# A convolution and soft-MoE kernel on one core: the last two output stores are issued as seven stores of fewer partitions

## The chip, the cores and the metric

The kernel runs on one NeuronCore of a Trainium2 chip. The metric is the device time of one execution in microseconds. The output goes from SBUF to HBM by DMAs that the SyncE engine (SP) issues on one queue; 16 DMA engines of the core carry them out.

## What is computed

An input `x` of 8 sequences of 3584 tokens with 192 channels goes through a dynamic convolution of 7 taps, whose weights are a softmax of `weight_gen` per token and head, and then through a soft mixture of experts with 32 slots. The lines that matter are these:

```python
w = softmax(weight_gen)                          # over the 7 taps
out = np.einsum('bshk,bskhg->bshg', w, x_unf)    # the convolution
...
logits = x @ phi
slot_input = softmax(logits, axis=0).T @ x       # dispatch: over all 28672 tokens
slot_out[e] = relu(slot_input[e] @ w1[e]) @ w2[e]
c = softmax(logits, axis=1)
return c @ slot_out                              # combine: 28672 x 192 floats
```

All of it is float32. The result is about 22 MB.

## The kernel before

The kernel has two long phases. In the first, up to about 229 us, the input is loaded, convolved on TensorE, transposed, multiplied with `phi`, and reduced into the slots. The loads of `x` go into 32 partitions each, those of the tap weights and of the expert weights into 128. Then a short middle part computes the experts.

The second phase writes the output. It is cut into 25 parts, listed by `out_order()`; the list is `parts`. A part is a piece of one batch (the first 128 channels, `kind` 0) or of two batches (their last 64 channels, `kind` 1) over 18 or 17 groups of 104 tokens. For each part `rows` makes the matmuls of TensorE (line 990), `evict` copies the four PSUM quarters into one region of SBUF (a `spot`) with ScalarE and VectorE (line 996), and `store` issues the DMA on SP (line 1001). A part after the first three is one store of 128 partitions, each partition one contiguous run of `4 * n * 26` floats: 7488 bytes for 18 groups, 7072 bytes for 17. The partition's runs lie behind one another in the output buffer, and the host puts them in order. The first three parts are two smaller stores each, so there are 28 stores.

A planner (`op`, `times`) sets the order of the instructions on the engines; on SP the stores go out in the order of `parts`. A store waits for the copies that fill its spot. Completion of a DMA is counted on one of eight semaphores in turn (called DMAHW0 to DMAHW7 below), and a DMA waits for the one that used its semaphore before, eight DMAs earlier. Behind the last store SP waits for all DMAs that are still out (line 1143), and then the program ends.

The function in question is `store`, with `j` the part's number, `n` its groups, and `lo`, `hi` its quarters; `left[0]` is the place in the output.

Of the kernel before, what the change touches and what calls it, by code (L numbers as in the profile page):

```python
# [17 lines left out]
T = 26  # L18
# [38 lines left out]
def conv_soft_moe(ctx, tc, xh, wh, phi, w1a, w1b, w2, out):  # L57
    nc = tc.nc
    V, A, G, P, SY = nc.vector, nc.scalar, nc.gpsimd, nc.tensor, nc.sync
# [639 lines left out]
    k = SLOTS - 2  # L699
# [125 lines left out]
    for i in sorted(range(len(ops)), key=lambda i: (at[i], i)):  # L825
        if ops[i][5] is loadw2 and ops[i][6] in later:
            continue
        n = len(block.instructions)
# [5 lines left out]
        elif ops[i][0] == SP and at[i] > PACED:  # L834
            to = max((t, k) for k, (t, _) in enumerate(steps) if t <= at[i])[1]
# [138 lines left out]
    spots = [w1flat[:, i * OW : (i + 1) * OW] for i in range(E * F // OW)]  # L974
# [5 lines left out]
    parts = list(out_order())  # L980
    pos, left = {}, [0]
# [12 lines left out]
    def evict(j, n, lo, hi, copy):  # L994
        to = spots[j % len(spots)][:, lo * n * T : hi * n * T]
        copy(to.rearrange("p (q c) -> p q c", c=n * T),  # L996
             pos[j][lo // 2][:, lo % 2 : lo % 2 + hi - lo, 0 : n * T])

    def store(j, n, lo, hi):
        w = (hi - lo) * n * T  # L1000
        SY.dma_start(out[128 * left[0] : 128 * (left[0] + w)].rearrange("(p c) -> p c", p=128),
                     spots[j % len(spots)][:, lo * n * T : hi * n * T])
        left[0] += w

    extra = []
# [20 lines left out]
    def turn_two():  # L1026
        twos[0] += 1
        return ("two", twos[0] % 4)

    for j, (kind, b, g, n) in enumerate(parts):  # L1030
        two, to = [turn_two(), turn_two()], ("spot", j % len(spots))
        op(TE, (1.1 + 0.8 * kind) * (n + 6) / 24, [("cT", 2 * (b + half) + (g >= STEPS[1][0])) for half in range(1 + kind)]
           + ["sob"] * kind, two, rows, kind, b, g, n, j)
        cuts = ((0, 2, AC), (2, 4, VE)) if j < 3 else ((0, 2, AC), (3, 4, VE), (2, 3, AC))
        free = ["w2"] * (j >= RESTAT + 2)
        for lo, hi, e in cuts:
            if e == AC:
                op(AC, 0.14 + 0.4 * (hi - lo) * n / 18, [two[lo // 2], *free], [(to, lo)], evict, j, n, lo, hi, A.copy)
            else:
                op(VE, 0.12 + 0.52 * (hi - lo) * n / 18, [two[1], *free], [(to, lo), ("ev", j)], evict, j, n, lo, hi, V.tensor_copy)  # L1040
        if 4 <= j + 2 < EARLY + 3:
            op(VE, 0.74, [("ev", j)], [("cT", j + 2)], turn, (j + 2) // 2, j % 2)
        for lo, hi in ((0, 2), (2, 4)) if j < 3 else ((0, 4),):
            op(SP, 0.576 * (hi - lo) * n / 18, [], [(to, c[0]) for c in cuts if lo <= c[0] < hi],
               store, j, n, lo, hi, late=2.0)
        if j == RESTAT:
            rest = turn_two()
            op(TE, 1.05, [], [rest], others, 0)
        elif j == RESTAT + 1:
            op(TE, 1.05, [], [rest, "w2"], others, 1)  # L1050
            op(AC, 0.22, [rest], ["sos"], lambda: A.copy(sos[:, DA:D], extra[0][:, 0]))
            op(TE, 0.4, ["sos"], [rest], other_sums)
            op(VE, 0.22, [rest], ["sob"], lambda: V.tensor_copy(sob, extra[0][:, 1]))
# [5 lines left out]
def out_order():  # L1059

    cut = ((0, 18), (18, 17))
    for kind, e in ((0, 0), (0, 1), (0, 2), (0, 3), (1, 0), (0, 4), (1, 2), (0, 5), (0, 6),
                    (1, 4), (0, 7), (1, 6)):
        for g, n in cut:
            if (kind, e, g) == (0, 0, 0):
                yield from ((0, 0, 0, 9), (0, 0, 9, 9))
            else:
                yield kind, e, g, n
# [79 lines left out]
```

## Time and profile before

| what | value |
|---|---|
| three runs | 296.55, 294.46, 296.4 us; median 296.4 us |
| span of the profiled execution | 295.2 us, from the first to the last instruction |
| the output phase | first store issued at 235.6 us, last one at 283.3 us |
| last copy into SBUF | ends at about 283.3 us |
| last bytes of the output leave | about 293.9 us |
| busy shares over the span | PE 88%, DVE 72%, ACT 61%, POOL 54% |

The profile's page gives the busy share of each engine over the whole span and, in 40 equal slices of 7.4 us, the busy share of the engines and of the 16 DMA engines in tenths. A packet in the DMA views is one contiguous run of a transfer, here one partition's row; packets of four bytes are the marks that a DMA engine writes when it has finished its share of a DMA.

### The profile page before, as it was taken

What the parts mean: (1) busy time and instruction counts of PE and PEld (TensorE: products, weight loads), DVE (VectorE), ACT (ScalarE), POOL (GpSimd) and SP (SyncE); (2) the same over time, 40 slices, a digit from 0 to 9 for tenths busy, and PEclk for the clock granted to TensorE, in tenths of its full rate; (3) what the DMA queues carried; (4) which work ended last, traced back from release to release, by engine and by line L of the source; (5) the groups of instructions that cost most, each with busy time, mean ns of one, the idle gap of its engine ahead of it and who ended that gap; (6) DMA issues with size and microseconds to landing.
All of it is one profiled execution on the core that took longest, in us unless ns stands there. A gap on an engine that the chain in (4) does not pass through costs nothing.

```text
span 295.2 us, 16119 instructions
## 1 busy us (share of the span) xinstructions
PE 259.5 (88%) x6996; PEld 210.5 (71%) x6996; DVE 213.2 (72%) x385; ACT 180.4 (61%) x307; POOL 160.1 (54%) x253
## 2 busy tenths in 40 slices
PE   8799999999999999989999999999999797956510
PEld 4578988998997898879899988888869552312100
DVE  8776988887997878676859787773278498977310
ACT  8866657665766666655575666665222378967430
POOL 9975858578686684656465736720036316454100
PEclk9999999999999999999999999999999999967775
DMA  6885776677767766775777758675889099999994
GB/s 188 231 221 154 222 213 188 174 229 199 217 171 228 198 196 178 228 201 161 197 219 220 207 162 232 196 205 168 277 267 297 15 370 414 418 415 414 415 420 174
DMA packets 31558, 70.11 MB, mean 237 GB/s; under 512 B 5888, under 2 KB 21248, under 8 KB 31488
## 3 DMA queue, kind: packets, MB, share of 16 engines
q1 hardware_dynamic: 31488, 69.08, 73.9%
q8 instruction: 55, 0.90, 1.3%
q14 instruction: 15, 0.12, 0.1%
HBM read 46.70 MB, written 22.36 MB: 234 GB/s over the span
## 4 chain that ended last, share of the span: by engine, by line
PE 77%; DMA 6%; issue 4%; DVE 4%; POOL 2%; ACT 2%; ACTq 0%; POOLq 0%; DVEq 0%
PE ring L263 34%; PE ring L283 17%; PE ls L339 8%; PE acb L417 8%; PE two L990 5%; DMA out<-big 4%; PE ring L900 2%; ACT big L996 1%; DMA big<-w 1%; DVE cT L475 1%; POOL LT L106 1%; PE ring L922 1%; POOL big L433 1%; DVE big L433 1%; PE acb L365 1%
## 5 line engine op out<-in xcount | busy, mean ns | idle before, releaser
L263 PE MATMUL ring<-big,band 128*26 128x96 f32 x4480 | 113.1, 248 | 4.8 <-issue 2.9
L263 PEld LDWEIGHTS ring<-big,band 128*26 128x26 f32 x4480 | 101.4, 130 | 15.4 <-issue 8.6
L271 ACT COPY tm<-ring 128x768 f32<-128x768 f32 x68 | 54.4, 800 | 63.2 <-PE ring L263 42.3
L236 DVE STREAM_TRANSPOSE band<-wide 128x832 f32<-128x832 f32 x70 | 70.5, 1025 | 3.8 <-POOL wide L227 2.5
L283 PE MATMUL ring<-ident,tm 122*128 122x122 f32 x408 | 50.5, 273 | 0.5 <-issue 0.5
L227 POOL TENSOR_TENSOR wide<-taps,sum 128x364 f32<-128x364 f32 x32 | 31.4, 982 | 26.6 <-DVE sum L218 13.5
L289 ACT COPY cm<-ring 128x624 f32<-128x624 f32 x68 | 44.1, 690 | 1.6 <-PE ring L283 1.4
L283 PEld LDWEIGHTS ring<-ident,tm 122*128 122x128 f32 x408 | 42.2, 141 | 3.5 <-issue 0.6
L196 POOL TENSOR_TENSOR taps<-taps,top 128x364 f32<-128x364 f32 x34 | 32.9, 974 | 4.3 <-DVE top L188 4.3
L212 POOL TENSOR_TENSOR si<-taps 128x208 f32<-128x208 f32 x34 | 21.7, 637 | 21.5 <-ACT taps L204 20.8
L990 PE MATMUL two<-cT,so 32*128 32x442 f32 (+2 forms) x136 | 22.3, 665 | 12.4 <-DVE cT L475 7.0
L188 DVE TENSOR_REDUCE top<-taps 128x52 f32<-128x364 f32 x34 | 27.8, 821 | 1.3 <-DMA taps<-wh 1.3
L417 PE MATMUL acb<-tm,dt 128*32 128x193 f32 x544 | 26.9, 328 | 0.7 <-issue 0.4
L339 PE MATMUL ls<-cm,phi_sb 128*32 128x208 f32 x544 | 27.4, 338 | 0.0
L94 POOL TENSOR_TENSOR LT<-LT,rm 128x576 f32<-128x576 f32 (+1 forms) x16 | 18.1, 1131 | 16.9 <-DVE rm L92 16.8
L106 POOL TENSOR_TENSOR LT<-LT,sm 128x576 f32<-128x576 f32 (+1 forms) x16 | 18.1, 1133 | 16.7 <-DVE sm L104 16.7
L990 PEld LDWEIGHTS two<-cT,so 32*128 32x128 f32 x136 | 8.6, 212 | 23.1 <-ACT big L996 6.5
L218 DVE RECIPROCAL sum<-sum 128x52 f32<-128x52 f32 (+1 forms) x36 | 16.4, 455 | 10.7 <-POOL sum L214 10.5
L204 ACT ACTIVATE taps<-taps 128x364 f32<-128x364 f32 (+1 forms) x36 | 17.8, 502 | 6.6 <-POOL taps L196 6.5
L339 PEld LDWEIGHTS ls<-cm,phi_sb 128*32 128x32 f32 x544 | 18.2, 109 | 3.7
L417 PEld LDWEIGHTS acb<-tm,dt 128*32 128x32 f32 x544 | 17.2, 110 | 4.9 <-issue 1.3
L346 DVE TENSOR_REDUCE mx<-ls 128x1 f32<-128x416 f32 x17 | 9.9, 585 | 14.6 <-PE ls L339 12.6
(135 smaller groups left out, 297.5 us busy)
## 6 DMA issues: line engine op xcount, KB each, us to landing
big<-xh SPq DMA_DIRECT2D x224, 120.0 KB, 3.5
taps<-wh SPq DMA_DIRECT2D x35, 182.0 KB, 3.6
out<-big SPq DMA_DIRECT2D x7, 884.0 KB, 9.8
big<-w SPq DMA_DIRECT2D x32, 192.0 KB, 3.9
out<-big SPq DMA_DIRECT2D x6, 936.0 KB, 10.4
w1a_sb<-w1a SPq DMA_DIRECT2D x32, 128.0 KB, 3.4
out<-w1a_sb SPq DMA_DIRECT2D x3, 936.0 KB, 12.1
w1b_sb<-w1b SPq DMA_DIRECT2D x16, 128.0 KB, 3.5
```

What stands on the lines that cost most here:

```text
L188: V.tensor_reduce(out=row(m), in_=run(c, 0, KT).rearrange("p k s -> p s k"), axis=AX.X, op=ALU.max)
L196: eng.tensor_tensor(out=t, in0=t, in1=rows7(tops.pop((c, 0))), op=ALU.subtract)
L212: eng.tensor_tensor(out=fold, in0=run(c, 0, 4), in1=run(c, 4, 8), op=ALU.add)
L227: eng.tensor_tensor(out=dst, in0=raw[c % NTAP][:, 0:KT], in1=m.unsqueeze(1).to_broadcast([128, KT, n, T]), op=ALU.mult)
L236: V.transpose(bands[c % NBAND][:, b].rearrange("p b j l -> p (b j l)"), wide[:, b].rearrange("p b j -> p (b j)"))
L263: P.matmul(cv[32 * blk : 32 * blk + T, p % 2, o : o + 4 * GW], bands[g // 8 % NBAND][:, g // 4 % CH, :, i], xbd[:, place(t), :, b * GW : ( ...
L271: copy(tms[tm_at(u)][:, pr + of.start : pr + of.stop, 1 : 2 * D + 1], cv[:, of, 0 : 2 * D])
L283: P.transpose(pt[:, j // 3, o : o + TR], tm[0:TR, pr + j // 3, 1 + o : 129 + o], ident[0:TR, 0:TR])
L289: copy(cm.rearrange("p (a i) (b j) -> p a (i b) j", i=3, j=T), pts["t", k][:, of, 0 : 3 * 128].rearrange("p a (i j) -> p a i j", j=32)[... ...
L339: P.matmul(lp[32 * blk : 32 * blk + 32, lo:hi, par, 0:T], phi_sb[:, 2 * par + i, :], cm[:, lo:hi, 1 if i else 2 * par, blk, :], start=(i = ...
L417: P.matmul(ac[32 * q : 32 * q + 32], dt[:, g, :], tm[:, g // 2, o : o + D + 1], start=(g < 4), stop=(g + 4 >= 2 * n))
L990: P.matmul(pos[j][q // 2][m * half : m * half + m, q % 2, 0 : n * T], of[32 * q : 32 * q + 32], cT[32 * q : 32 * q + 32, g0 : g0 + n, 0:T] ...
```

## The change

The last two parts are stored in pieces. The last but one (part 23, rows of 7488 bytes) goes out as 120 partitions and then the remaining 8; the last one (part 24, rows of 7072 bytes) as 64, 30, 14, 12 and 8. The bytes, their places and the order of partitions are the same; every other store stays one DMA of 128 partitions.

```diff
+    SHARES = {len(parts) - 2: (120, 8), len(parts) - 1: (64, 30, 14, 12, 8)}
+
     def store(j, n, lo, hi):
         w = (hi - lo) * n * T
-        SY.dma_start(out[128 * left[0] : 128 * (left[0] + w)].rearrange("(p c) -> p c", p=128),
-                     spots[j % len(spots)][:, lo * n * T : hi * n * T])
+        to = out[128 * left[0] : 128 * (left[0] + w)].rearrange("(p c) -> p c", p=128)
+        p = 0
+        for k in SHARES.get(j, (128,)):
+            SY.dma_start(to[p : p + k], spots[j % len(spots)][p : p + k, lo * n * T : hi * n * T])
+            p += k
         left[0] += w
```

The order of instructions differs on SP alone, at the end of the program. Before, the last stores on SP stand so (partitions x floats, and the semaphores that each waits for, without their values):

```order
363 L1001 DMA out<-big 128x1872 [waits DMAHW2_49,Activation_49]
364 L1001 DMA out<-big 128x1768 [waits DMAHW3_49,Activation_49]
365 L1001 DMA out<-big 128x1872 [waits DMAHW4_49,Activation_49]
366 L1001 DMA out<-big 128x1768 [waits DMAHW5_49,Activation_49]
367 L1001 DMA out<-big 128x1872 [waits DMAHW6_49,Activation_49]
368 L1001 DMA out<-big 128x1768 [waits DMAHW7_49,Activation_49]
369 L1143 UNCONDITIONAL_BRANCH
```

Now the same place in the program reads:

```order
363 L1006 DMA out<-big 128x1872 [waits DMAHW2_49,Activation_49]
364 L1006 DMA out<-big 128x1768 [waits DMAHW3_49,Activation_49]
365 L1006 DMA out<-big 128x1872 [waits DMAHW4_49,Activation_49]
366 L1006 DMA out<-big 128x1768 [waits DMAHW5_49,Activation_49]
367 L1006 DMA out<-big 120x1872 [waits DMAHW6_49,Activation_49]
368 L1006 DMA out<-big 8x1872 [waits DMAHW7_49]
369 L1006 DMA out<-big 64x1768 [waits DMAHW0_49,Activation_49]
370 L1006 DMA out<-big 30x1768 [waits DMAHW1_49]
371 L1006 DMA out<-big 14x1768 [waits DMAHW2_49]
372 L1006 DMA out<-big 12x1768 [waits DMAHW3_49]
373 L1006 DMA out<-big 8x1768 [waits DMAHW4_49]
374 L1148 UNCONDITIONAL_BRANCH
```

Two stores became seven. The last three pieces wait for the semaphores DMAHW2 to DMAHW4, that is for the completion of the stores in rows 363 to 365 of the same list; nothing else moved on any engine.

## Rows read from the trace of the kernel before

**Rows 1.** The page: span; the 40 slices of DMA share and rate

```profile
span 295.2 us, 16119 instructions
...
DMA  6885776677767766775777758675889099999994
GB/s 188 231 221 154 222 213 188 174 229 199 217 171 228 198 196 178 228 201 161 197 219 220 207 162 232 196 205 168 277 267 297 15 370 414 418 415 414 415 420 174
```

**Rows 2.** Stretches: start:end, length, engines' busy us, PEclk, DMA share, GB/s

```profile
250.00:281.00 31.00, 20.34 (x166) 6.70 (x160) 21.36 (x39) 22.69 (x40) 13.08 (x12) 0.78 1.01 416
281.00:288.00 7.00, 0.23 (x8) 0.00 (x0) 0.91 (x2) 2.25 (x4) 0.00 (x0) 0.70 1.01 416
288.00:290.30 2.30, 0.00 (x0) 0.00 (x0) 0.00 (x0) 0.00 (x0) 0.00 (x0) 0.50 1.04 428
290.60:291.30 0.70, 0.00 (x0) 0.00 (x0) 0.00 (x0) 0.00 (x0) 0.00 (x0) 0.50 0.27 112
292.50:293.80 1.30, 0.00 (x0) 0.00 (x0) 0.00 (x0) 0.00 (x0) 0.00 (x0) 0.50 0.07 27
293.90:295.20 1.30, 0.00 (x0) 0.00 (x0) 0.00 (x0) 0.00 (x0) 0.00 (x0) 0.50 0.00 0
```

**Rows 3.** Waits on SP from 283 us: in total, times, longest

```profile
SPq L1143 <- DMA out<-big: 10.5, 5, 2.3
```

**Rows 4.** DMA packets in 290.3:290.6, 291.3:291.45, 292.1:292.45, 293.8:294.5 us; marks: under 512 B

```profile
DMA packets 17, 0.04 MB, mean 143 GB/s; under 512 B 11, under 2 KB 11, under 8 KB 17
DMA packets 4, 0.02 MB, mean 144 GB/s; under 512 B 1, under 2 KB 1, under 8 KB 4
DMA packets 5, 0.01 MB, mean 40 GB/s; under 512 B 3, under 2 KB 3, under 8 KB 5
DMA packets 1, 0.00 MB, mean 0 GB/s; under 512 B 1, under 2 KB 1, under 8 KB 1
```

**Rows 5.** DMA in 292.45:294.5 us: packets, MB; share of 16 engines

```profile
DMA packets 6, 0.04 MB, mean 17 GB/s; under 512 B 1, under 2 KB 1, under 8 KB 6
...
q1 hardware_dynamic: 6, 0.04, 4.2%
```

**Rows 6.** The same four counts one store earlier: 288.2:288.42, 289.1:289.25, 290.0:290.28, 291.6:291.8 us

```profile
DMA packets 26, 0.11 MB, mean 488 GB/s; under 512 B 11, under 2 KB 11, under 8 KB 26
DMA packets 12, 0.08 MB, mean 524 GB/s; under 512 B 1, under 2 KB 1, under 8 KB 12
DMA packets 20, 0.12 MB, mean 431 GB/s; under 512 B 3, under 2 KB 3, under 8 KB 20
DMA packets 4, 0.02 MB, mean 106 GB/s; under 512 B 1, under 2 KB 1, under 8 KB 4
```

**Rows 7.** DMA in 271.5:273 and in 280.2:281.2 us: the queues of instruction fetches

```profile
q8 instruction: 1, 0.02, 3.7%
...
q14 instruction: 1, 0.01, 1.9%
```

**Rows 8.** The stores from `big` on SP: count, issue in ns (min/median/max), first and last start

```profile
L1001 SPq DMA_DIRECT2D out<-big x13: 332/332/421, 246.6 to 283.3; - x13
```

**Rows 9.** DMA issues at 275.3, at 283.3, and in 235:236.5 us: KB, us to landing

```profile
out<-big SPq DMA_DIRECT2D x1, 936.0 KB, 12.4
out<-big SPq DMA_DIRECT2D x1, 884.0 KB, 11.1
...
out<-w1a_sb SPq DMA_DIRECT2D x2, 234.0 KB, 2.4
```

**Rows 10.** DMA in 5:11 us: packets; share of 16 engines; what was issued

```profile
DMA packets 679, 1.41 MB, mean 236 GB/s; under 512 B 167, under 2 KB 399, under 8 KB 679
...
q1 hardware_dynamic: 679, 1.41, 86.6%
...
big<-xh SPq DMA_DIRECT2D x10, 120.0 KB, 3.3
```

**Rows 11.** DMA in 222:229 us: share of 16 engines; what was issued

```profile
q1 hardware_dynamic: 1500, 2.05, 89.4%
...
big<-w SPq DMA_DIRECT2D x7, 192.0 KB, 4.2
```

## Prediction

> **What bounds the kernel now.** I read the page's slices first: from the 33rd slice on, the 16 DMA engines are 90% busy or more and move 414 to 420 GB/s, until the last slice, where share and rate fall to 4 tenths and 174 GB/s [rows 1]. So the end belongs to the stores. The view by stretches says the same more closely: from 250 to 290.3 us the DMA share is 1.01 to 1.04 (a full queue on every engine), and from 288 us no compute engine does anything [rows 2]. Then the tail is not full: 0.27 of 16 engines, about four, are at work from 290.6 to 291.3 us, 0.07 (one engine) from 292.5 to 293.8 us, none after 293.9 us. SP meanwhile only waits for DMAs, 10.5 us in five waits, at the line behind the program [rows 3]. What sets the end is thus not the amount of output but the slowest of the 16 engines.
>
> How uneven they are can be counted from the marks, packets of four bytes that an engine writes when its share of a store is done. Of the last store's 16 marks, 11 come by 290.6 us, one by 291.45, three by 292.45, and one after 293.8 [rows 4]. One store earlier the same count is 11, 1, 3 and 1, with the last 3.3 to 3.5 us behind the first [rows 6], so these lags are there before the last two stores and no longer grow. Some lag comes from instruction fetches on the same engines: a 16 KB one at about 272 us took 3.7% of 16 engines over 1.5 us, or 0.89 us of one engine, and one more falls between 280.2 and 281.2 us [rows 7]. No row gives an engine a name.
>
> **The price of a row.** After the three late marks one engine moves five rows of 7072 bytes and its mark: 4.2% of 16 engines over 2.05 us [rows 5] is 1.38 us, so 0.275 us a row; in proportion 0.291 us for 7488 bytes. Alone it is no faster than the average engine was under full load: 416 GB/s over 1.01 times 16 engines is 25.7 GB/s, or 0.275 us for 7072 bytes [rows 2]. So a row taken off the last engine shortens the end by that much, and one put on an engine that is in time costs nothing while it stays ahead of the last.
>
> **What the pieces do.** A store of 128 rows gives each of 16 engines 8 rows: its 16 marks are counted above. No transfer in this trace has a number of rows that 16 doesn't divide, so how 120, 30, 14, 12 and 8 rows are dealt is not shown. Two ends bound it: equal shares on the largest number of engines, up to 16, that divides the rows, always beginning at the same first engine; or a spread over all 16 as even as it can be. The second moves at most a row from one engine to another, 0.3 us either way. I take the first, because every transfer that the trace has gives equal shares. Then the 120 rows leave out engine 16, the 8 go one each to engines 1 to 8, the 64 go four to each, the 30 two each to 1 to 15, and the 14, 12 and 8 one each to the first 14, 12 and 8. Over both stores engines 1 to 8 get 18 rows in place of 16, engines 9 to 12 still 16, engines 13 and 14 15, engine 15 14, and engine 16 four. [...]
>
> In time: engine 16 loses 8 rows of 0.291 and 4 of 0.275, 3.43 us. Engines 1 to 8 gain one row of each, 0.57 us. Engines 13 and 14 lose 0.28 us and engine 15 loses 0.55 us.
>
> **The sum.** I take the one that ends at 293.9 us to be engine 16. That is a choice: one engine stands clearly apart, by the same distance two stores running [rows 4, 6], and a lasting handicap fits a fixed place at an end of the deal better than one in its middle. It then ends at 293.9 - 3.4 = 290.5 us. The three that end by 292.4 us are next. If places are evenly likely among the fifteen left, at least one of the three lies among the first eight with 1 - (7 x 6 x 5)/(15 x 14 x 13) = 0.92, so the end is 292.4 + 0.57 = 293.0 us. From the last mark to the end of the span take the same 295.2 - 293.9 = 1.3 us [rows 1, 2] (the landing of the last mark, SP's last wait, the closing barrier). The span becomes 294.3 us, 0.9 us less. Were all three outside the first eight it would be 293.7 us, and with perfectly even ends (0.9 + 3 x 1.8 + 3.4 = 9.7 us of lag, 0.6 us on each of 16) 292.4 us: that is the most there is to win.
>
> **What the extra DMAs cost.** SP issues five more. An issue takes 332 to 421 ns [rows 8], so 1.7 to 2.1 us in all; work in the queue hides them, since the last store is issued at 283.3 us and lands 11.1 us later [rows 9]. The last piece also waits for the semaphore of the store issued at 275.3 us, which lands 12.4 us later [rows 9], at 287.7 us. A store onto idle queues lands 2.4 us after its issue, its data's time included [rows 9], so this piece could be done by 287.7 + 0.4 + 2.4 = 290.5 us; engines 1 to 8 reach its row no sooner than 290.6 + 0.57 - 0.28 = 290.9 us. The margin of 0.4 us is a lower bound. If the cover were gone each us of lateness would show on engines 1 to 8 alone, which are ahead of the 293.0 us end by 1.8 us, except a late one. Five more sets of marks take about 0.01 us each; behind the pieces on SP stands only the closing wait.
>
> **Rival A, the last engine is not the one relieved.** Then the end moves with its place: 293.9 + 0.57, a span of 295.8 us, if it is one of the first eight; 295.2 us on 9 to 12; 294.7 to 294.9 us on 13 to 15. An even spread of the pieces belongs here, 294.9 to 295.5 us. For it: no row names the engine. Against it: the lasting lag. [...]
>
> **Rival B, rows of few partitions go slower.** This is the one that ends slower than before. The trace's transfers into 32 partitions, with few others between, carry 1.41 MB in 6 us at 86.6% of 16 engines, 17.0 GB/s an engine [rows 10]; loads into 128 partitions 2.05 MB in 7 us at 89.4%, 20.5 GB/s [rows 11]; stores from 128 25.7 GB/s [rows 2]. So few partitions may cost a factor of 1.20 (against other loads) up to 1.51 (against stores). Engines 1 to 8 move one row of 0.291 and nine of 0.275 us in such pieces, 2.77 us; the factor adds 0.55 to 1.4 us. The end becomes 293.6 to 294.4 us and the span 294.9 to 295.7 us. It decides from a factor of 1 + 0.9/2.77 = 1.33. If 120 partitions are slowed as well, 8 x 0.291 us adds another 0.5 to 1.2 us, up to 296.9 us. Against it: the 32-partition rows are loads with their own latency, and the late engines move their last rows when others have finished. [...]
>
> **How the numbers follow.** The forecast has 0.5, rival A 0.27, rival B 0.23. The profiled span of 295.2 us is 1.2 us below the median of the runs, 296.4 us; I carry the difference over, so 294.3 becomes 295.5 us. The low end is that of even ends, 2.8 us less than before: 296.4 - 2.8 = 293.6 us, which also covers the lowest run of before less the 0.9 us. The high end is rival A's or B's 0.5 to 0.6 us above before: 297.0 us. Left out are the slowed 120 partitions. A measurement of this kernel can tell about 1%, 3 us, from no change; the largest possible gain is 2.8 us, so faster by over 1% gets 0.06, slower by over 1% (B with more than its rows show) 0.04, and within 1% 0.90.
>
> **What would show it.** In the profile after: marks of the last pieces within about 2.5 us rather than 3.5; one engine alone at the end for less than 0.7 us; SP's closing waits shorter; the last issue near 287.8 us. Rival A shows as a single engine still alone past 293.5 us; rival B as more time per row from 288.5 us on, a DMA share near 1 with a rate under 350 GB/s. I am wrong if the fetches fall on other engines in each execution, which changes the second-latest group, or if the lag of the last engine is not lasting at all.

## Result and the profile after

The change makes the kernel slower: 300.95 us median against 295.97 us for the kernel before, and a ratio of 1.0138 with a 95% interval of 1.0096 to 1.018. Timed again beside the experiments it was 1.0163 (1.0086 to 1.0241). The forecast was 295.5 us, within 293.6 and 297.0 us; the measurement lies about 4 us above that range.

Ratios compare executions in the faster of this kernel's two states and medians are over all of them; three profiles are of slower executions: the first of the change, that of the cut in the middle and that of both stores in halves. The first profile of the change was late before the stores too (its last whole store is issued at 283.5 us, before at 280.1 us), so below times run from the landing of an unchanged store to the end, and a second profile of the same kernel ("again") stands beside it.

These are the page's span and slices of the change, which answer to [rows 1], first of the first profile, then of the second:

```profile
span 302.5 us, 16124 instructions
...
DMA  6967776676667865776578666775896299999992
GB/s 184 221 191 188 199 214 196 186 214 187 199 183 212 220 188 161 213 216 183 162 216 218 202 179 204 216 209 167 259 293 223 87 407 417 417 416 411 415 319 81
```

```profile
span 298.4 us, 16124 instructions
...
DMA  6967867577857676776677777666995399999992
GB/s 181 227 184 191 223 191 209 167 219 211 220 142 230 194 223 177 212 214 203 176 192 236 213 202 214 185 186 202 293 290 180 125 410 414 417 417 415 413 320 79
```

The last slice but one still shows 9 tenths in the DMA row, yet its rate is 319 or 320 GB/s where its neighbours move over 410. Busy engines move less. The stretches of the second profile (start:end, length, busy time of the engines, PEclk, DMA share, GB/s) answer to [rows 2]:

```profile
250.00:281.00 31.00, 20.61 (x160) 6.72 (x160) 21.53 (x38) 22.89 (x40) 12.88 (x12) 0.74 1.02 417
281.00:286.00 5.00, 0.55 (x8) 0.00 (x0) 0.62 (x1) 1.91 (x4) 0.00 (x0) 0.84 1.02 411
286.30:288.00 1.70, 0.00 (x0) 0.00 (x0) 0.00 (x0) 0.00 (x0) 0.00 (x0) 0.50 0.97 282
288.00:290.00 2.00, 0.00 (x0) 0.00 (x0) 0.00 (x0) 0.00 (x0) 0.00 (x0) 0.50 0.98 290
294.00:296.00 2.00, 0.00 (x0) 0.00 (x0) 0.00 (x0) 0.00 (x0) 0.00 (x0) 0.50 0.13 46
296.00:297.40 1.40, 0.00 (x0) 0.00 (x0) 0.00 (x0) 0.00 (x0) 0.00 (x0) 0.50 0.04 15
```

Until 286 us nothing differs from before: 411 to 417 GB/s at a share of 1.02. From 286.3 us, when the engines that are in time come to the 120 rows, the share stays near 1 and the rate is 282 to 290 GB/s. Over the tail one engine is left again (0.04 of 16 over 1.4 us is 0.9 us of one engine, which has finished by 297.0 us). The DMA view of 295.48 to 297 us shows what it does, and answers to [rows 5]:

```profile
DMA packets 10, 0.04 MB, mean 23 GB/s; under 512 B 5, under 2 KB 5, under 8 KB 10
...
q1 hardware_dynamic: 10, 0.04, 5.7%
```

Five rows and five marks: the mark of its share of the 64, two rows and a mark of the 30, and one row and one mark each of the 14, 12 and 8. An engine with a row of the piece of 8 is one of eight: in the first profile eight late completions, from 298.20 to 301.44 us, stand behind one at 297.04 us, which comes as the issue of that piece ends (296.88 us). These eight, wherever they sit, are the first eight below. In the first profile the same count from 299.6 to 301.2 us reads 10 packets with five marks, too. So the engine that ends last was not relieved of twelve rows; it was given two. It is the engine that was last before the cuts: in both profiles its rows can be followed backwards packet by packet, with gaps under 0.1 us, to its share of the last whole store, which lands last there too.

The issues of the last stores, listed by size for 274 to 293 us of the second profile (KB each, us to landing), answer to [rows 9]; the issue times of the ten stores from 276 us on in the first profile answer to [rows 8]:

```profile
out<-big SPq DMA_DIRECT2D x1, 884.0 KB, 10.3
out<-big SPq DMA_DIRECT2D x1, 877.5 KB, 12.6
out<-big SPq DMA_DIRECT2D x1, 442.0 KB, 12.6
out<-big SPq DMA_DIRECT2D x1, 207.2 KB, 11.9
```

```profile
L1006 SPq DMA_DIRECT2D out<-big x10: 332/926/3427, 277.1 to 296.2; - x10
```

The 884.0 KB store is the last whole one, 877.5 KB are the 120 rows, 442.0 KB the 64 and 207.2 KB the 30. An issue takes up to 3.4 us in place of 0.42 us, and the last piece is issued at 296.2 us rather than the 287.8 us of the prediction. SP's closing wait for DMAs (the row below, from 280 us on in the second profile) is shorter than in [rows 3] for that reason alone: SP itself comes to it late.

```profile
SPq L1148 <- DMA out<-big: 4.2, 2, 3.9
```

**The yardstick.** With landings read as issue plus time to landing, and per store as the last of the 16 completions, the tail of each profiled execution falls into three steps. "Last but three" and so on count the parts; a cut part lands with its last piece.

| kernel | last but three to last but two | to last but one | to last | sum, us |
|---|---|---|---|---|
| before | 2.22 | 2.28 | 2.16 | 6.66 |
| the change | 3.28 | 4.03 | 2.87 | 10.18 |
| the change, again | 2.61 | 4.54 | 2.84 | 9.99 |
| last but one as 120, 8 | 2.16 | 3.77 | 2.17 | 8.10 |
| last as 64, 30, 14, 12, 8 | 2.20 | 2.31 | 2.48 | 6.99 |
| last as 64, 64 | 2.17 | 2.33 | 2.16 | 6.66 |
| last but one as 112, 16 | 2.20 | 3.61 | 2.16 | 7.97 |
| last as 64, 32, 16, 8, 4, 2, 1, 1 | 2.17 | 2.34 | 2.22 | 6.73 |
| last as 8 times 16 | 2.20 | 2.37 | 2.36 | 6.93 |
| last in 8 pieces of columns | 2.25 | 2.59 | 2.61 | 7.45 |
| last as 64, 49, 7, 7, 1 | 2.16 | 2.32 | 3.54 | 8.02 |
| last as 120, 8 | 2.18 | 2.32 | 2.43 | 6.93 |
| both as 64, 64 | 2.19 | 2.32 | 2.17 | 6.68 |

The change adds 3.3 to 3.5 us to this tail, 1.1 to 1.2% of the span, which lies inside both measured intervals. Steps of whole stores agree among kernels to 0.1 us, except 2.59 us beside the pieces of columns and 2.61 and 3.28 us in the change. Each line of the table is one execution: the two of the change differ by up to 0.7 us in a step, and a step also holds the delay from an engine's mark to its landing, about 0.50 us beside whole stores and 0.34 us in the tail of the change. So a difference of 0.3 us between two lines is at the edge of what the table can tell; one of 1 us is well clear of it. The timed ratios, with intervals of 0.35% (1 us) and more to either side, tell less.

### The profile page after: what moved, and what is told of

Same layout as the page of the kernel before. It is cut to its first block, busy times and chain, and to the rows that moved or that the text cites. A ratio compares the mean times of both kernels' runs of the same rounds, so it can differ in the third digit from the quotient of the medians.

```text
span 302.5 us, 16124 instructions
## 1 busy us (share of the span) xinstructions
PE 261.3 (86%) x6996; PEld 210.8 (70%) x6996; DVE 213.2 (70%) x385; ACT 180.6 (60%) x307; POOL 160.0 (53%) x253
## 5 line engine op out<-in xcount | busy, mean ns | idle before, releaser
L990 PE MATMUL two<-cT,so 32*128 32x442 f32 (+2 forms) x136 | 21.5, 639 | 12.1 <-DVE cT L475 3.8
L339 PEld LDWEIGHTS ls<-cm,phi_sb 128*32 128x32 f32 x544 | 17.4, 109 | 4.3
## 6 DMA issues: line engine op xcount, KB each, us to landing
out<-big SPq DMA_DIRECT2D x6, 884.0 KB, 9.7
```

Source lines behind the costliest of these rows:

```text
L339: P.matmul(lp[32 * blk : 32 * blk + 32, lo:hi, par, 0:T], phi_sb[:, 2 * par + i, :], cm[:, lo:hi, 1 if i else 2 * par, blk, :], start=(i = ...
L990: P.matmul(pos[j][q // 2][m * half : m * half + m, q % 2, 0 : n * T], of[32 * q : 32 * q + 32], cT[32 * q : 32 * q + 32, g0 : g0 + n, 0:T] ...
```

## Experiments

Three theories stood against one another. **P**: rows whose partitions lie close together wait for one another when several engines read them. **L**: the last engine is one of the first eight and merely has more rows. **S**: the pieces are issued too late. Unless something else is said, a diff is against the kernel with the change, and only its lines that differ are shown.

### Each cut alone

The last but one alone:

```diff
-    SHARES = {len(parts) - 2: (120, 8), len(parts) - 1: (64, 30, 14, 12, 8)}
+    SHARES = {len(parts) - 2: (120, 8)}
```

> Only the last store but one is cut, as 120 and 8; the last stays whole. Yardstick: the time from the landing of the last store but two to the landing of the last store, 4.4 us before and 6.9 us with both stores cut. Theory P (rows whose partitions lie close together wait for one another): the 120 rows cost the last engine 3.7 us in place of 2.3, so 4.4 + 0.3 + 1.4 = 6.1 us and a ratio near 1.006. Theory L (the last engine is one of the first eight and only gets more rows): 4.4 + 0.3 = 4.7 us, ratio 1.001. Theory S (the pieces are issued too late, since SP takes 1.2 to 3.4 us for each): one extra issue is hidden, 4.4 to 4.7 us, ratio 1.000.

Ratio 1.0033 (0.995 to 1.0117). The tail is 8.10 us, and 5.94 us from the landing of the last but two, near the 6.1 us of P. The 120 rows land 3.48 us behind the store before them on the last engine, in place of 2.28 us, though it moves the same eight rows; its row of the 8 adds 0.29 us. Followed packet by packet, the eight rows take 0.29, 0.29, 0.29, 0.56, 0.29, 0.57, 0.59 and 0.73 us: half of them are as fast as alone, the others take twice as long and more. The stretches of this kernel show the fall of the rate at a high share:

```profile
282.00:284.50 2.50, 0.00 (x0) 0.00 (x0) 0.00 (x0) 0.00 (x0) 0.00 (x0) 0.75 1.01 417
286.50:288.00 1.50, 0.00 (x0) 0.00 (x0) 0.00 (x0) 0.00 (x0) 0.00 (x0) 0.50 0.87 297
```

The last alone:

```diff
-    SHARES = {len(parts) - 2: (120, 8), len(parts) - 1: (64, 30, 14, 12, 8)}
+    SHARES = {len(parts) - 1: (64, 30, 14, 12, 8)}
```

> Only the last store is cut, as 64, 30, 14, 12 and 8. P: the 64 rows cost the last engine 0.4 us more, the small pieces nothing on it, since the other engines are done by then: 4.4 + 0.3 + 0.4 = 5.1 us, ratio 1.002; but rows of 0.5 to 1.0 us on the other engines. L: 4.7 us, ratio 1.001. S: the last piece is issued some 8 us after the first, near 291.5 us, and the engines that are in time wait for it; 4.4 to 5.5 us, ratio 1.000 to 1.004.

Ratio 1.0027 (0.9958 to 1.0097), tail 6.99 us; from the landing of the last but two 4.79 us, nearer to L (4.7) than to P (5.1). The last engine's four rows of the 64 take 1.12 us, so nothing slows it there and P's 0.4 us did not come, although it is not alone: 0.46 of 16 engines, about seven, are at work in that stretch.

```profile
291.60:292.75 1.15, 0.00 (x0) 0.00 (x0) 0.00 (x0) 0.00 (x0) 0.00 (x0) 0.50 0.46 160
```

S's late issue did not come either: SP issues the last piece at 287.3 us, and the last engine's marks for the pieces of 14, 12 and 8 come 0.26 to 0.28 us apart, a row's time each.

### Equal shares, so that only the dealing differs

```diff
-    SHARES = {len(parts) - 2: (120, 8), len(parts) - 1: (64, 30, 14, 12, 8)}
+    SHARES = {len(parts) - 1: (64, 64)}
```

> Only the last store is cut, as 64 and 64: each of 16 engines still has eight rows, four from each half. P: eleven engines move two times four rows at half rate, so their last marks come 1 to 2 us later than before against the store ahead of it (3.3 to 4.4 us in place of 2.2); the last engine, alone for its last rows, loses at most 0.5 us: 4.4 to 4.9 us, ratio 1.000 to 1.002. L and S: 4.4 us and marks as before, ratio 1.000.

Ratio 1.0005 (0.9936 to 1.0074), tail 6.66 us, as before. The end is untouched, yet the engines that are in time are slowed as P said: while they move the first half, all 16 engines together run at 267 and 241 GB/s.

```profile
285.00:288.00 3.00, 0.00 (x0) 0.00 (x0) 0.00 (x0) 0.00 (x0) 0.00 (x0) 0.67 0.99 406
288.40:289.40 1.00, 0.00 (x0) 0.00 (x0) 0.00 (x0) 0.00 (x0) 0.00 (x0) 0.50 1.08 267
289.40:290.20 0.80, 0.00 (x0) 0.00 (x0) 0.00 (x0) 0.00 (x0) 0.00 (x0) 0.50 0.82 241
```

Read packet by packet, 17 of the 46 rows of the last store that start between 288.4 and 290.2 us take 0.26 to 0.31 us, 14 take 0.50 to 0.60 us and 8 take 0.70 to 0.80 us: once, twice or nearly three times the time alone. Before, 1118 of 1138 rows between 270 and 290 us take 0.26 to 0.31 us.

```diff
-    SHARES = {len(parts) - 2: (120, 8), len(parts) - 1: (64, 30, 14, 12, 8)}
+    SHARES = {len(parts) - 2: (112, 16)}
```

> Only the last store but one is cut, as 112 and 16: equal shares, seven rows and one on each of 16 engines, so nothing is taken off any. [...] L and S: 4.4 us, ratio 1.000.

Ratio 1.0005 (0.9918 to 1.0092), tail 7.97 us; from the landing of the last but two 5.77 us, where L and S had 4.4. The 112 rows are seven on every engine by the equal shares that the completions of the next cut show, and the last engine needs 3.30 us for its seven, where seven rows of 0.291 us are 2.0 us. While all 16 engines are busy the rate is well under 400 GB/s:

```profile
286.60:288.00 1.40, 0.00 (x0) 0.00 (x0) 0.00 (x0) 0.00 (x0) 0.00 (x0) 0.50 0.98 347
288.00:289.00 1.00, 0.00 (x0) 0.00 (x0) 0.00 (x0) 0.00 (x0) 0.00 (x0) 0.50 1.12 350
```

So neither 120 rows nor a share on only 15 engines (15 late completions in the first profile of the change) is needed for the loss, nor a row more on the last engine. The timed ratio did not show these 1.3 us; the trace's step does.

### Where the last engine sits

```diff
-    SHARES = {len(parts) - 2: (120, 8), len(parts) - 1: (64, 30, 14, 12, 8)}
+    SHARES = {len(parts) - 1: (64, 32, 16, 8, 4, 2, 1, 1)}
```

> Only the last store is cut, as 64, 32, 16, 8, 4, 2, 1 and 1 rows, to find the last engine's place and how pieces are dealt. If a piece goes in equal shares to the first engines, the pieces of 8, 4, 2 and 1 rows have 8, 4, 2 and 1 late marks. If the last mark of the piece of 8 comes about 3.5 us behind the first, the last engine is one of the first eight; if the same holds for the pieces of 4, 2 and 1, it is one of the first four, the first two, the first. Theory L needs at least the first. [...] Theory S says that SP takes over 1 us for each issue of the pieces.

One execution. The late completions of the pieces number 16, 16, 16, 8, 4, 2, 1 and 1, so shares are equal: on 16 engines, and with fewer than 16 rows on as many engines as there are rows. Each mark of the piece of 4 lands 0.25 to 0.28 us behind one of the piece of 8, and each of the piece of 2 as far behind one of the piece of 4, so a smaller piece goes to a part of the same engines. The view of 291.85 to 292.6 us holds the last three marks of the execution and two rows:

```profile
DMA packets 5, 0.01 MB, mean 19 GB/s; under 512 B 3, under 2 KB 3, under 8 KB 5
...
q1 hardware_dynamic: 5, 0.01, 4.9%
```

They land at 292.38, 292.66 and 292.93 us as the last of the pieces of 32, 16 and 8. The piece of 4 had landed whole by 292.08 us. The last engine has a share of the 8 and none of the 4: counted in the order of the deal, it is one of engines 5 to 8.

```diff
-    SHARES = {len(parts) - 2: (120, 8), len(parts) - 1: (64, 30, 14, 12, 8)}
+    SHARES = {len(parts) - 1: (64, 49, 7, 7, 1)}
```

> Only the last store is cut, as 64, 49, 7, 7 and 1 rows. With equal shares on the first engines, every engine gets 4 rows of the 64, the first seven get 7 + 1 + 1 more (the very first one more), and engines 8 to 16 none. The binary cut left engines 5 to 8 as the place of the last one. If it is engine 8, its last mark is that of the 64 rows, 1.1 us behind its mark for the store before, in place of 2.2: it lands 1.1 us earlier, and the end is set by the first seven, at 3.3 to 4.7 us after the landing of the last store but two (4.4 us before); ratio 0.996 to 1.001. If it is engine 5, 6 or 7, it has 13 rows in place of 8: 4.4 + 1.4 = 5.8 us or more, ratio 1.005.

Ratio 1.0081 (1.0037 to 1.0125), tail 8.02 us; 5.86 us from the landing of the last but two, the 5.8 us of the second case. The last engine's mark for the 64 lands at 292.74 us, that of the 49 at 294.64 us: 1.90 us for seven rows. From 294 to 295 us the view shows its three remaining marks, of 49, 7 and 7, with a row before each of the last two:

```profile
DMA packets 5, 0.01 MB, mean 14 GB/s; under 512 B 3, under 2 KB 3, under 8 KB 5
```

So it is engine 5, 6 or 7 and not engine 8, if the place is the same in both executions, which ran on different chips. The hope of a better version, relieving engine 8 alone, fell with it.

### Does it matter that others are reading?

```diff
-    SHARES = {len(parts) - 2: (120, 8), len(parts) - 1: (64, 30, 14, 12, 8)}
+    SHARES = {len(parts) - 8: (120, 8)}
```

> The same cut of 120 and 8, but on the store seven places earlier, with the stores behind it whole. P: while it is moved the rate falls from 416 to 260 to 300 GB/s, every engine that has a share of it loses 1.0 to 1.5 us, and since the queue is full to the end nothing is won back: ratio 1.003 to 1.006. L: only the extra row counts, 0.3 us: ratio 1.001. S: one extra issue with a full queue, ratio 1.000.

Ratio 1.0005 (0.9952 to 1.0058), which neither shows nor excludes a loss of up to 1.7 us. In its profile the last engine needs 4.29 us for the 120 rows and 0.37 us for the row of the 8, and then 15.8 us for the seven whole stores behind them, 2.26 us each, as ever: 2.4 us are lost and not won back. That execution took 301.9 us, where the kernel's median is 298.2 us, and the timed runs do not bear out so much, so the size in the middle stays uncertain.

```diff
-    SHARES = {len(parts) - 2: (120, 8), len(parts) - 1: (64, 30, 14, 12, 8)}
+    SHARES = {len(parts) - 1: (120, 8)}
```

> The cut of 120 and 8 on the last store, where the last engine works alone for most of its share. P: the 120 rows, which cost it 3.5 to 3.7 us in the last store but one, cost 2.2 to 2.6 us here, and the engines in time lose 0.5 to 2 us each, as there; from the landing of the last store but two to the end 4.7 to 5.1 us. L: 4.4 + 0.3 = 4.7 us. If the price of 120 rows lay in the dealing itself and not in the neighbours, it would again be 3.5 us: 6 us.

One execution, tail 6.93 us, 4.75 us from the landing of the last but two. The 120 rows that cost the last engine 3.48 us in the last store but one cost it 2.17 us here. The stretches show why: while the others are at it the share is 0.91 and the rate 294 GB/s, and from 292.6 us hardly more than two engines are left.

```profile
289.30:292.00 2.70, 0.00 (x0) 0.00 (x0) 0.00 (x0) 0.00 (x0) 0.00 (x0) 0.50 0.91 294
292.60:294.90 2.30, 0.00 (x0) 0.00 (x0) 0.00 (x0) 0.00 (x0) 0.00 (x0) 0.50 0.15 58
```

The price is therefore not in the cut of 120 and 8 by itself; it is paid only while other engines read. This is the run that decides against a price of the dealing alone. Company alone is not enough, either: the last engine moved the whole store ahead of it at 0.28 to 0.29 us a row while the others were in the 120 rows. P's reason, that rows wait because their partitions lie close together, fits both and the rows that take twice or three times as long; that it is the partitions in SBUF and not, for example, the places in HBM is argued, not shown.

### Many pieces: issue or neighbours?

```diff
-    SHARES = {len(parts) - 2: (120, 8), len(parts) - 1: (64, 30, 14, 12, 8)}
+    SHARES = {len(parts) - 1: 8 * (16,)}
```

> Only the last store is cut, into eight pieces of 16 partitions: each engine still has eight rows, one in each piece, so no engine gets more or less. [...] L: no change, ratio 1.000. S: seven extra issues of 1.2 to 3.4 us, 8 to 24 us: the last piece is issued after 291 us; ratio 1.00 to 1.03. [...]

Ratio 1.0023 (0.9988 to 1.0058), tail 6.93 us: the store lands 0.2 us later (2.36 us in place of 2.16). The rate does not fall further as the pieces get smaller: all 16 engines together run at 238 and 277 GB/s, much as with halves of 64 (267 and 241); 41 of the 91 rows of this store that start between 286.5 and 289.5 us take 0.26 to 0.31 us:

```profile
283.00:285.50 2.50, 0.00 (x0) 0.00 (x0) 0.00 (x0) 0.00 (x0) 0.00 (x0) 0.70 1.03 424
286.50:287.50 1.00, 0.00 (x0) 0.00 (x0) 0.00 (x0) 0.00 (x0) 0.00 (x0) 0.50 0.93 238
287.50:288.50 1.00, 0.00 (x0) 0.00 (x0) 0.00 (x0) 0.00 (x0) 0.00 (x0) 0.50 1.06 277
```

That engines drift apart and read different pieces at the same moment would fit; it was not tried by itself.

```diff
-    SHARES = {len(parts) - 2: (120, 8), len(parts) - 1: (64, 30, 14, 12, 8)}
+    SPLIT = {len(parts) - 1: 8}
...
-        p = 0
-        for k in SHARES.get(j, (128,)):
-            SY.dma_start(to[p : p + k], spots[j % len(spots)][p : p + k, lo * n * T : hi * n * T])
-            p += k
+        m = SPLIT.get(j, 1)
+        c = (hi - lo) * n * T // m
+        for i in range(m):
+            SY.dma_start(to[:, i * c : (i + 1) * c],
+                         spots[j % len(spots)][:, lo * n * T + i * c : lo * n * T + (i + 1) * c])
```

> Only the last store is cut, into eight pieces of 128 partitions and an eighth of the columns, 884 bytes a row: as many DMAs as with eight times 16 partitions, but all partitions in each. P: no row waits for a neighbour, 64 short rows an engine at 0.04 us, 2.6 us in place of 2.2: 4.4 to 4.9 us, ratio 1.000 to 1.002, and issues of SP as before, near 0.33 us. S: issues cost by their number, so as slow as the eight pieces of 16 partitions. L: no change.

Ratio 1.0007 (0.9959 to 1.0056), tail 7.45 us. With all 128 partitions in each piece the rate of the 16 engines is 329 GB/s, well above the 238 to 277 GB/s of as many pieces of 16 partitions, though its rows are an eighth as long. And no row waits for another: 524 of the 525 rows of this store that start between 288.6 and 290.6 us take 0.03 to 0.06 us. So the rows that take twice as long come with pieces of few partitions and not with many pieces.

```profile
288.60:290.60 2.00, 0.00 (x0) 0.00 (x0) 0.00 (x0) 0.00 (x0) 0.00 (x0) 0.50 0.94 329
...
L1007 SPq DMA_DIRECT2D out<-big x9: 332/829/1252, 282.2 to 292.8; - x9
```

The second row is SP's issues: up to 1.25 us for pieces of 128 partitions as well, so P's 0.33 us was wrong and a longer issue does not need pieces of few partitions; what causes it was not tried. The last piece is issued at 292.8 us, once the store eight DMAs before it has landed, but the last engine did not wait for it: its short rows follow one another without a gap. Most of the 0.8 us is the short rows themselves: 64 of them with eight marks take the last engine 2.85 us in place of 2.16 us. In the 2.59 us of the step before, its rows take 0.29 to 0.31 us; there the delay from mark to landing has grown from 0.57 to 0.79 us.

### Both stores, equal and again

```diff
-    SHARES = {len(parts) - 2: (120, 8), len(parts) - 1: (64, 30, 14, 12, 8)}
+    SHARES = {len(parts) - 2: (64, 64), len(parts) - 1: (64, 64)}
```

> Both last stores are cut in halves of 64 partitions: every engine keeps its eight rows of each store, nothing is taken off any, and two DMAs more are issued. P: the engines in time need 4 to 4.5 us for each store in place of 2.2 to 2.3, so they are still reading when the last engine gets to its rows, which then meet neighbours too: from the landing of the last store but two to the end 5 to 7 us in place of 4.4; ratio 1.002 to 1.008. L: 4.4 us, ratio 1.000.

Ratio 1.0034 (0.998 to 1.0088), tail 6.68 us: a miss for P, which said 5 to 7 us from the last but two, where it was 4.49. All 16 engines fall to 253 GB/s (DMA share 0.92 from 288.9 to 290.5 us), but the last engine keeps its 2.2 to 2.3 us a store, 0.27 to 0.30 us a row, although the others still read beside it (a share of 1.00 until 293 us).

```profile
288.90:290.50 1.60, 0.00 (x0) 0.00 (x0) 0.00 (x0) 0.00 (x0) 0.00 (x0) 0.50 0.92 253
290.50:293.00 2.50, 0.00 (x0) 0.00 (x0) 0.00 (x0) 0.00 (x0) 0.00 (x0) 0.50 1.00 346
```

So what meets the last engine may depend on which partitions the others read in that moment. With halves they may always be in the other half; this is argued, not shown.

The change itself, once more:

> The change as it is, both stores cut, beside the others on the same chip. Yardstick: from the landing of the last store but three to the landing of the last one, 6.7 us before, 10.2 us in the first profile of the change, 8.1 us with the last but one cut alone, 7.0 us with the last cut alone. If the two cuts simply add, 8.4 us and a ratio near 1.006. If they make each other worse (engines that are in time are held up by the small pieces, so that they still read the neighbours of the last engine's rows while it works through its backlog), 9.5 to 10.5 us and a ratio of 1.010 to 1.016 again.

Ratio 1.0163 (1.0086 to 1.0241), tail 9.99 us. The two cuts do not simply add (8.43 us). The table tells where the rest is: the whole store ahead of the cuts takes the last engine 2.61 and 3.28 us in place of 2.22; the 120 rows take 4.25 and 3.73 us where the cut alone had 3.48; the 64 rows 1.46 and 1.48 us where the cut alone had 1.12. Row by row it is the same picture as before: rows of 0.28 us stand beside others of 0.5 to 0.9 us, among the 120 rows and the last rows of the whole store ahead, and one of the four rows of the 64 takes 0.7 us. Whether both cuts together cause the first two, or single executions vary that much, stays open; for the 120 rows the 4.29 us in the middle, with whole stores behind them, fit the latter.

## Why the prediction was wrong

**What bounds the kernel, and the price of a row: right.** The end was and is the slowest of 16 engines, and a row that it moves alone takes what was said: 0.27 to 0.29 us for each late piece of one row.

**How rows are dealt: right.** The pieces of the change, 120, 8, 64, 30, 14, 12 and 8 rows, have 15, 8, 16, 15, 14, 12 and 8 late completions in the first profile, those of the cut into 64, 32, 16, 8, 4, 2, 1 and 1 rows 16, 16, 16, 8, 4, 2, 1 and 1. In each case that is the largest number up to 16 that divides the rows, and the smaller pieces of the binary cut go to a part of the same engines. Which numbers those engines have no run shows.

**Which engine is last: wrong, and this is the first step that failed.** "I take the one that ends at 293.9 us to be engine 16" rested on one engine standing apart, and on a guess that such an engine sits at an end of the deal. It stands apart in every profile, but in all that tell its place it is among the first eight, and the two that tell more leave engines 5 to 7. The term was -3.43 us and had to be +0.57 us. That is rival A, whose span of 295.8 us is already longer than the 295.2 us of before; it had 0.27 where, without a row that names an engine, the eight places out of 16 that gain rows deserved about half.

**What rows of few partitions cost: the effect that rival B names was right, its size too small, its cover wrong.** The prediction held that "the late engines move their last rows when others have finished". For the last store cut alone that comes out (1.12 us for four rows of the 64; 2.17 us for eight of the 120, with hardly more than two engines at work). For the one before it is false. An engine that is 3.4 us behind is a store and a half behind, so while it moves the 120 rows the others are still reading, and some of its rows then take two or three times as long. In the full change this reaches the last rows of the whole store ahead as well. The 120 rows cost it 1.2 to 2.0 us more, against "another 0.5 to 1.2 us", and this term was the one left out of the range.

**Two rivals that exclude nothing were treated as if one replaced the other.** What each took in the second profile: 0.57 us for two rows more, 4.25 - 2.28 = 1.97 us for the 120, 2.61 - 2.22 = 0.39 us for the store ahead of it, 1.46 - 1.10 = 0.36 us for the 64 (four rows of 0.275 us), in all 3.3 us; 9.99 - 6.66 = 3.33 us is measured. These are parts of one trace and must add up; the two cuts tried alone account for 1.8 us of it (8.43 - 6.66), and the rest is seen only with both. The prediction's own upper prices, 0.57 + 1.4 + 1.2 us, would have given 3.2 us, but by luck: its 1.4 us for the small pieces measured 0.36 us, its 1.2 us for the 120 rows 1.97 us.

**What the extra DMAs cost: the price was wrong, and the conclusion held by luck.** "332 to 421 ns" an issue became up to 3.4 us, and the last piece was issued at 296.2 us in the first profile. But the last engine's one-row pieces follow each other a row's time apart, at 296.80, 297.07 and 297.34 us in the second one, so it never waited for SP. The engines in time did, and had the last engine been relieved this might have been the next bound: in the second profile the other marks of the piece of 8 land by 295.2 us, 2.2 us ahead of the end.

**Offsets.** The runs that list both show the device time about 2 us above the span (304.48 and 302.5 us), not the 1.2 us that was carried over from a profile and the median of other executions.

**What would show it.** A "DMA share near 1 with a rate under 350 GB/s" was the sign of rival B and came at once, and so did rival A's, a single engine still alone past 293.5 us. A shorter closing wait on SP came too and meant nothing of the kind, since SP arrived there later.

No version here beats the kernel before. What could be won was at most 2.8 us by the prediction's count. The cuts that touch the last store alone left the tail as it was or made it longer, and a deal that starts at the same engines for every piece, as the completions show it here, cannot leave out engines 5 to 7 and still use those behind them.

## What to carry to other kernels

When one of many equal workers ends last, find out which one it is before taking work off it: a cut into 8, 4, 2 and 1 rows narrowed its place to four of 16 in one execution. A store that was cut by partitions moved the same bytes here but not in the same time, as long as other engines were still reading; test each cut at the place where it will stand, since the same 120 rows cost 1.2 to 2.0 us with stores behind them and nothing in the last store. Rivals that can all be true at once are added, not weighed against one another.

## What was not expected of the hardware

SP's issue of a DMA took 0.33 us with whole stores in the queue and up to 3.4 us where pieces followed each other, for pieces of 128 partitions too (up to 1.25 us). With stores of 64 partitions the 16 engines together move 241 to 267 GB/s while most of them are at it, and with eight pieces of 16 partitions 238 to 277 GB/s, hardly different. Rows that are slowed do not stretch a little: with the last store in halves, 17 of 46 rows take 0.26 to 0.31 us, and of the other 29, 22 take 0.50 to 0.60 or 0.70 to 0.80 us, twice or nearly three times as long.

The engine that ends last lands 3.5 to 3.6 us behind the first in every store of the tail before, and the lag is passed on from store to store. It does not come from one event: in the trace of before the last landing of a store is 2.5 us behind the first at 264 us, the gap grows by 0.05 to 0.2 us a store to 3.5 us at 283 us, and then it stays. One of the three engines that are 1.8 us behind came there in one step, in the store that was under way during the 16 KB instruction fetch at 271.8 us. What makes the last engine slow stays open.
